# Attention scores with queries on partitions in place of keys, in a kernel of cluster attention and token mixing

## The chip, the cores and the metric

The kernel runs on one core of a Trainium2 chip. Its engines work side by side and each goes through its own queue of instructions in order: TensorE (PE; its weight loads are shown apart as PEld), VectorE (DVE), ScalarE (ACT), GpSimd (POOL), and SyncE (SP), which here only issues DMA transfers. The metric is the time of one execution on the device, in microseconds (us).

## The reference

Attention runs over 4 batches of 8 heads, 768 positions, 64 features. Queries and keys attend to one another only where both fall into the same one of 16 clusters of their head. The result, 4 x 768 x 512, goes through a mixer.

```python
q_assign = argmax(einsum('bhsd,hcd->bhsc', q_n, c_n))      # k_assign likewise
mask = q_assign[:, :, :, None] == k_assign[:, :, None, :]
scores = where(mask, scale * q @ k.T, -1e9)
scores = scores - max(scores, axis=-1)
attn = exp(scores)
attn = attn / (sum(attn, axis=-1) + 1e-09)
x = (attn @ v), heads side by side                          # (4, 768, 512)
theta = x @ w_theta
y = w_tok_r @ (x * cos(theta)) + w_tok_i @ (x * sin(theta))   # over positions
u = x + y
out = u + maximum(u @ w_ch, 0.0)
```

## The kernel before

**Two phases.** The attention fills the first 527 us, the mixer the rest. The attention goes over 16 pairs (a batch and two heads j = 0, 1), each in 12 units (`NU`), 192 in all.

**Scores.** A unit is one half `a` of the queries (384) by one key tile `i` (128 keys), for both heads. Scores stand transposed: keys on partitions, queries along the free axis (`scores`, L358). The products keep close to full float32 precision from parts: q and k are cut into a rounded part `hi` and a remainder `lo` (L297, L302), and SP spreads rows of these over the tiles `t1q`, `t2q`, `t1k`, `t2k` (`spread`, L308, 16 transfers a pair). Two matmuls then make one score tile `sc`: t1 over 112 rows, t2 over 128. Of the 112, 16 are the one-hot rows of the clusters, with a large constant, so that scores between different clusters are far below the others.

**The row of maxima.** With queries along the free axis the maximum over keys isn't at hand on any one engine. So the scores of queries by keys are also computed the other way round, from t1 alone, 11 units ahead (`LEAD`; `row_max`, matmul to `m` L329), and DVE takes the maximum of 768 (L333). These columns are transposed (`shift_row`, tile `mt`, L341), copied to `mr` and sent by SP into row 64 of `t2q` (L345, "t2q<-mr"), where a row of ones in `t2k` subtracts them from the scores by the matmul itself.

**After the scores.** ACT takes the exponential of 128x384 twice a unit into `at` (L362). POOL adds the `at` of the key tiles up in `acc` (L368). Three units later, every second unit, PE does the weighted sums of two units, `av` (L408), straight from `at`, since keys are on partitions as the product needs it. After the pair's last unit PE sums `acc` over partitions by a column of ones (`sums`, L377), and the sums go to DRAM (sd), back as 128 x 12 (sq), through DVE's reciprocal, to DRAM again and back as rows broadcast over partitions (rb): L388, L391, L395, L398, all on SP. POOL multiplies (`normalise`, L420), and the result goes to DRAM for the mixer.

**Preparation.** `assign` loads raw q and k of a pair (L224), makes the clusters' logits `lg` (L230), transposes them (`lt`, L239), takes maxima and one-hot rows on DVE, transposes them back (`ot`, L260), and SP puts the rows of `oht` into t1q and t1k (L268). Three sets of t tiles allow this two pairs ahead. Four weight matrices arrive as 64-bit floats; `to_f32` and `split_w` (L110 to L148) turn a chunk into float32 by four operations on ACT and DVE (L127 to L135) and into hi and lo on ACT and POOL. w_theta, a third of the token weights and w_ch are converted during the attention (`early_weights`), the others at the start of the mixer (`late`).

**The order.** The program is written unit by unit. Helpers that belong to a later unit wait in `todo` until it comes (`at_unit`, `stages` with one unit for each stage of a generator). `in_order` then chains all instructions of a unit to those of the unit before, engine by engine, so that each engine works in this order; SP is so chained only up to unit 5 (`SPU`), and after it in the order that the scheduler gives.

**Mixer.** `theta` (xp, tp, kk, r, ab, zh, zl) for each of 6 position tiles of 4 batches, `mix` (y, L672), `channel` (cp and cy, L695). The first channel matmul of the first batch comes 82 us after the last av; until then the late weights are converted.

Of the kernel before, what the change touches and what calls it, by code (L numbers as in the profile page):

```python
# [21 lines left out]
LEAD = 11  # L22
SPU = 6
A2 = (-4, 1, 3, 6, 8)
PRE = 4
PW = 256
TAIL = 2
WARM = 2
SUMS = (2, 2, 5, 8)
EARLY = 2  # L30
LAG = 3
NAT = 5
# [10 lines left out]
def kernel(  # L43
# [21 lines left out]
    P = 128  # L65
# [36 lines left out]
    ecol = cpool.tile([P, 32], F32, name="ecol")  # L102
    nc.vector.memset(ecol, 0.0)
    nc.vector.memset(ecol[:, 0:1], 1.0)


# [3 lines left out]
    def to_f32(src, cols, new):  # L110
# [17 lines left out]
        nc.vector.tensor_scalar(  # L128
# [30 lines left out]
    w_c = [hi_lo(wpool, f"wch{c}", DM) for c in range(NCT)]  # L159
# [14 lines left out]
    p3 = actx.enter_context(tc.tile_pool(name="p3", bufs=3))  # L174
    pw = actx.enter_context(tc.tile_pool(name="pw", bufs=2))
    p2 = actx.enter_context(tc.tile_pool(name="p2", bufs=2))
    p1 = actx.enter_context(tc.tile_pool(name="p1", bufs=1))
# [36 lines left out]
    def assign(pi):  # L214
# [5 lines left out]
        for n, src, eng in (("q", qT, nc.sync), ("k", kT, nc.scalar if pi == 0 else nc.sync)):  # L220

            raw = pw.tile([P, S], F32, tag="w64" if pi == 1 else "raw", name=f"raw{n}{pi}")
            st.setdefault(pi, dict(tsets[pi % 3]))["raw" + n] = raw
# [34 lines left out]
        for t in range(NT):  # L258
# [4 lines left out]
            out=oht, in_=ot, func=AF.Identity, scale=msc[0:4 * C], bias=mbi[0:4 * C])  # L263
        s = st[pi]
        for j in range(2):
            for n, x in enumerate(("t1q", "t1k")):
                g = 2 * C * n + C * j
                nc.sync.dma_start(out=f(s[x][96:96 + C, j]), in_=f(oht[g:g + C]))  # L268
# [3 lines left out]
    last_exp, last_acc, last_sum, last_load = ([None] for _ in range(4))  # L272
    KM = 96 + C

    def load_v(pi):
# [9 lines left out]
        q=(("t1q", 0, "hi", 0, 64), ("t1q", 64, "hi", 0, 32), ("t2q", 0, "lo", 0, 64), ("t2q", 96, "hi", 32, 32)),  # L285
        k=(("t1k", 0, "hi", 0, 64), ("t1k", 64, "lo", 0, 32), ("t2k", 0, "hi", 0, 64), ("t2k", 96, "lo", 32, 32)))


    for x in range(3):
        nc.gpsimd.memset(f(tsets[x]["t2q"][64:96]), 0.0)  # L290
        nc.gpsimd.memset(f(tsets[x]["t2k"][64:96]), 0.0)
        nc.gpsimd.memset(f(tsets[x]["t2k"][64:65]), 1.0)

    def part_hi(pi, n):
        s = st[pi]
        s["hi" + n] = pe.tile([P, S], F32R, tag="hi" + n, name=f"hi{n}{pi}")
        nc.scalar.copy(out=s["hi" + n], in_=s["raw" + n])  # L297

    def part_lo(pi, n, eng):
        s = st[pi]  # L300
        s["lo" + n] = s["raw" + n].bitcast(F32R)
        eng.tensor_tensor(out=s["lo" + n], in0=s["raw" + n], in1=f(s["hi" + n]), op=ALU.subtract)  # L302

    def spread(pi, n):
        s = st[pi]
        for to, row, part, first, rows in ROWS[n]:
            for j in range(2):
                nc.sync.dma_start(  # L308
                    out=f(s[to][row:row + rows, j]), in_=f(s[part + n][64 * j + first:64 * j + first + rows]))

    NU = 2 * NT

    def split_u(u):
        pi, x = divmod(u, NU)
        return (pi,) + divmod(x, NT)

    def row_max(u, c):


        pi, a, i = split_u(u)  # L320
        s = st[pi]
        t, j = divmod(i, 2)
        t += a * NT // 2
        if i == 0 and c == 0:
            s["nm", a] = p2.tile([P, 2, NT // 2], F32, tag="nm", name=f"nm{u}")
        if c == 0:
            s["m"] = ps0.tile([P, 2, 512], F32, tag="m", name=f"m{u}")
        m = s["m"]
        nc.tensor.matmul(  # L329
            m[:, c, 0:HS], lhsT=s["t1q"][0:KM, j, t * P:(t + 1) * P],  # L330
            rhs=s["t1k"][0:KM, j, c * HS:(c + 1) * HS], start=True, stop=True)
        if c == 1:
            nc.vector.tensor_reduce(  # L333
                out=s["nm", a][:, j, i // 2:i // 2 + 1], in_=m[:, :, 0:HS], op=ALU.max, axis=AX.XY,
                negate=True)

    def shift_row(pi, a):

        s = st[pi]
        mt = bank(f"mt{pi}{a}")[0:NT, 0:P]  # L340
        nc.tensor.transpose(out=mt, in_=s["nm", a].rearrange("p j t -> p (j t)"), identity=identf)  # L341
        mr = p2.tile([NT, P], F32R, tag="mr", name=f"mr{pi}{a}")
        nc.scalar.copy(out=mr, in_=mt)
        for j in range(2):
            (nc.scalar if pi == a == 0 else nc.sync).dma_start(  # L345
                out=f(s["t2q"][64:65, j, a * HS:(a + 1) * HS]).rearrange("o (t n) -> o t n", n=P),
                in_=f(mr[j * NT // 2:(j + 1) * NT // 2]))

    def scores(u, j):

        pi, a, i = split_u(u)
        s = st[pi]
        if j == 0:
            s["at", a, i] = p3.tile([P, 2, HS], F32, tag="at", name=f"at{u}", bufs=NAT)
        at = s["at", a, i]
        sc = bank(f"sc{u}_{j}")[:, 0:HS]
        for x, z, kk in (("t1k", "t1q", KM), ("t2k", "t2q", P)):
            nc.tensor.matmul(  # L358
                sc, lhsT=s[x][0:kk, j, i * P:(i + 1) * P],
                rhs=s[z][0:kk, j, a * HS:(a + 1) * HS],  # L360
                start=(x == "t1k"), stop=(x == "t2k"))
        last_exp[0] = nc.scalar.activation(out=at[:, j], in_=sc, func=AF.Exp, scale=SCALE)  # L362
        if j == 1:
            if i == 1:
                s["acc", a] = p2.tile([P, 2, HS], F32, tag="acc", name=f"acc{u}", bufs=3)
            if i > 0:
# [435 lines left out]
```

## Time and profile before

| | us |
|---|---|
| median of 3 runs | 879.95 (874.2 to 884.32) |
| the profiled execution | 885.43 |
| its span, first to last instruction | 883.6 |
| first matmul for maxima | 27.5 |
| first exp | 49.6 |
| last av of the attention begins | 524.1 (sixteen matmuls, 2.8) |
| first channel matmul of the first batch | 609.1 |

The profile is that of one execution. Its page lists for each group of instructions the busy time, the mean of one, and the idle time of the engine just before them with what ended most of it. Matmuls overlap, so the distance between their starts tells what one costs, more than its own duration. PEclk is the share of TensorE's clock that was granted; its mean over the execution was 0.959. The chain of waits is followed back from the last instruction of a window, at each step to what released it.

### The profile page before, as it was taken

The page shows a single profiled execution, that of the slowest core. Times are in us where ns is not written, and L with a number is a line of the kernel's source. Part 1 is how long each engine was busy: PE and PEld are TensorE (multiplying, and loading weights), DVE is VectorE, ACT ScalarE, POOL GpSimd, SP SyncE. Part 2 cuts the span into 40 slices and gives each one's busy share as a digit, 9 for nine tenths or more (in the row PEclk, how much of TensorE's full clock was granted, in tenths as well). Part 3 has the DMA queues.
Part 4 walks back from the last instruction along what each step waited for, and adds up shares of the span by engine and source line. Part 5 has one row for each costly group of instructions (what it writes and reads, how often), then busy time and mean ns, then how long its engine had stood idle before and what let it go on. Part 6 is the DMA issues. An engine that isn't in the chain of part 4 may idle for free.

```text
span 883.6 us, 12635 instructions
## 1 busy us (share of the span) xinstructions
PE 807.2 (91%) x4509; PEld 599.7 (68%) x4509; DVE 511.6 (58%) x664; ACT 400.6 (45%) x790; POOL 545.8 (62%) x337
## 2 busy tenths in 40 slices
PE   2699998998798898899899999889999999999998
PEld 0366555555565564565556658679988988899998
DVE  4486776766766776678465439995333432344222
ACT  2156653654555564466545565544233323332220
POOL 7177887988978987899788777466122412241231
PEclk9999998998988998999899999999999999999999
DMA  5875768655845754755563113520400040001002
GB/s 143 217 203 148 186 144 203 172 172 154 189 141 146 209 154 108 201 149 165 127 159 124 37 52 121 172 87 1 143 1 1 1 143 1 1 26 47 1 7 67
DMA packets 45903, 99.87 MB, mean 113 GB/s; under 512 B 12944, under 2 KB 17808, under 8 KB 45456
## 3 DMA queue, kind: packets, MB, share of 16 engines
q1 hardware_dynamic: 45684, 98.66, 40.4%
q8 instruction: 36, 0.59, 0.3%
q10 hardware_dynamic: 156, 0.40, 0.1%
q14 instruction: 27, 0.22, 0.1%
HBM read 45.25 MB, written 12.78 MB: 66 GB/s over the span
## 4 chain that ended last, share of the span: by engine, by line
PE 66%; DMA 9%; DVE 8%; POOL 6%; issue 5%; SPq 3%; ACT 2%; ACTq 0%; POOLq 0%; DVEq 0%
PE y L672 18%; PE sc L358 13%; PE av L408 11%; PE tp L605 6%; PE m L329 5%; PE cy L695 4%; POOL acc L368 3%; SPq L308 3%; DMA t2q<-mr 2%; PE cp L695 2%; DMA sd<-se 2%; DMA t1q<-hiq 1%; DMA rawk<-in_kT_dram 1%; DVE wtmp L135 1%; PE lg L230 1%
## 5 line engine op out<-in xcount | busy, mean ns | idle before, releaser
L362 ACT ACTIVATE at<-sc 128x384 f32<-128x384 f32 x384 | 182.0, 491 | 164.3 <-PE sc L358 152.7
L333 DVE TENSOR_REDUCE nm<-m 128x1 f32<-128x768 f32 x192 | 182.4, 953 | 125.8 <-PE m L329 121.3
L368 POOL TENSOR_TENSOR acc<-acc,at 128x768 f32<-128x768 f32 x128 | 242.3, 1893 | 20.0 <-ACT at L362 12.7
L358 PE MATMUL sc<-t2q,t2k 128*128 128x384 f32 x384 | 138.9, 362 | 36.6 <-DMA t2q<-mr 36.6
L408 PE MATMUL av<-at,vt 128*64 128x384 f32 x768 | 155.7, 530 | 0.0
L358 PE MATMUL sc<-t1q,t1k 112*128 112x384 f32 x384 | 147.6, 384 | 0.0
L329 PE MATMUL m<-t1k,t1q 112*128 112x384 f32 x384 | 141.8, 370 | 5.8 <-DMA t1k<-oht 4.8
L626 POOL TENSOR_TENSOR zlc<-ab,zhc 128x512 fp32r<-128x512 f32 x24 | 32.6, 1359 | 158.4 <-ACT zhc L624 158.2
L358 PEld LDWEIGHTS sc<-t1q,t1k 112*128 112x128 f32 x384 | 76.1, 198 | 54.0 <-issue 32.3
L358 PEld LDWEIGHTS sc<-t2q,t2k 128*128 128x128 f32 x384 | 76.6, 200 | 43.7 <-DMA t2q<-mr 43.6
L408 PEld LDWEIGHTS av<-at,vt 128*64 128x64 f32 x768 | 48.9, 142 | 63.6 <-issue 63.3
L368 POOL TENSOR_TENSOR acc<-at,at 128x768 f32<-128x768 f32 x32 | 59.1, 1848 | 51.4 <-ACT at L362 51.4
L329 PEld LDWEIGHTS m<-t1k,t1q 112*128 112x128 f32 x384 | 80.3, 209 | 9.1 <-issue 6.6
L609 DVE TENSOR_SCALAR kk<-tp 128x512 int32<-128x512 f32 x24 | 16.6, 690 | 99.1 <-PE tp L605 99.1
L686 POOL TENSOR_TENSOR ul<-xT,uh 128x384 fp32r<-128x384 f32 (+1 forms) x36 | 33.5, 956 | 38.1 <-ACT uh L685 35.8
L672 PE MATMUL y<-wi_lo,zhs 128*128 128x512 f32 (+1 forms) x216 | 52.3, 320 | 2.6 <-POOL wi_lo L145 2.6
L672 PE MATMUL y<-wi_hi,zhs 128*128 128x512 f32 (+1 forms) x216 | 52.4, 321 | 1.2 <-ACT wi_hi L144 1.2
L672 PE MATMUL y<-wr_hi,zhc 128*128 128x512 f32 (+1 forms) x216 | 53.0, 323 | 0.0
L672 PE MATMUL y<-wr_lo,zhc 128*128 128x512 f32 (+1 forms) x216 | 52.7, 322 | 0.0
L672 PE MATMUL y<-wr_hi,zlc 128*128 128x512 f32 (+1 forms) x216 | 52.6, 322 | 0.0
L672 PE MATMUL y<-wi_hi,zls 128*128 128x512 f32 (+1 forms) x216 | 52.5, 322 | 0.0
L600 ACT COPY xn<-xp 128x512 f32<-128x512 f32 x24 | 14.0, 585 | 83.5 <-PE xp L598 83.5
(140 smaller groups left out, 1398.6 us busy)
## 6 DMA issues: line engine op xcount, KB each, us to landing
rawq<-in_qT_dram SPq DMA_DIRECT2D x16, 384.0 KB
t1k<-hik SPq DMA_DIRECT2D x32, 192.0 KB
t2k<-hik SPq DMA_DIRECT2D x32, 192.0 KB
t1q<-hiq SPq DMA_DIRECT2D x32, 192.0 KB
t2q<-rawq SPq DMA_DIRECT2D x32, 192.0 KB
vt<-in_v_dram SPq DMA_DIRECT2D x16, 384.0 KB
rb<-sd SPq DMA_DIRECT2D x32, 192.0 KB
xT_d<-xt SPq DMA_DIRECT2D x16, 384.0 KB
```

The costliest lines, as they stand in the source:

```text
L308: nc.sync.dma_start(out=f(s[to][row:row + rows, j]), in_=f(s[part + n][64 * j + first:64 * j + first + rows]))
L329: nc.tensor.matmul(m[:, c, 0:HS], lhsT=s["t1q"][0:KM, j, t * P:(t + 1) * P], rhs=s["t1k"][0:KM, j, c * HS:(c + 1) * HS], start=True, stop= ...
L333: nc.vector.tensor_reduce(out=s["nm", a][:, j, i // 2:i // 2 + 1], in_=m[:, :, 0:HS], op=ALU.max, axis=AX.XY, negate=True)
L358: nc.tensor.matmul(sc, lhsT=s[x][0:kk, j, i * P:(i + 1) * P], rhs=s[z][0:kk, j, a * HS:(a + 1) * HS], start=(x == "t1k"), stop=(x == "t2k"))
L362: last_exp[0] = nc.scalar.activation(out=at[:, j], in_=sc, func=AF.Exp, scale=SCALE)
L368: last_acc[0] = nc.gpsimd.tensor_tensor(out=s["acc", a], in0=prev, in1=at, op=ALU.add)
L408: nc.tensor.matmul(s["av"][64 * j:64 * j + 64], lhsT=s["vt"][:, i, j, :], rhs=s["at", a, i][:, j], start=(i == 0), stop=(i == NT - 1))
L605: nc.tensor.matmul(tp, lhsT=xx[:, c, :], rhs=w_th[c][k], start=(n == 0), stop=(n == 3 * NCT - 1))
L626: nc.gpsimd.tensor_tensor(out=zl, in0=tr, in1=zh.bitcast(F32), op=ALU.subtract)
L672: nc.tensor.matmul(y_at(b, d, c0, c1), lhsT=zz[:, d * P:(d + 1) * P], rhs=ww[:, c0:c1], start=first and lead, stop=last, skip_group_check= ...
L686: nc.gpsimd.tensor_tensor(out=ul[:, d, :], in0=x, in1=uh[:, d, :].bitcast(F32), op=ALU.subtract)
L695: nc.tensor.matmul(cp, lhsT=w_c[d][k][:, e * P:(e + 1) * P], rhs=uu[:, d, :], start=(n == 0), stop=(n == 3 * NCT - 1), skip_group_check=True)
```

## The change

Scores stand with queries on partitions. A unit is a query tile `t` of a half `a` and one head `j`: four matmuls make 128 queries by 768 keys in a tile `m` of two banks (L344). DVE takes its maximum into a column (L353), ACT takes one exponential over 128x768 with this column as its bias and writes the sums of its rows beside it (L362). The separate matmuls for maxima, the shift row with its transfers, the additions on POOL and the sums on PE are gone. t2 has 96 rows in place of 128. Since the bias comes after the scale, POOL multiplies raw q by the scale beforehand (`scale_q`).

For the weighted sums keys have to be on partitions, so PE transposes the exponentials (`turn`, L375): twelve blocks of 128x128 for two units, into three banks (tr), which ACT (two) and DVE (one) copy to `aT`. The weighted sums (L388) follow a half later, one key tile of both heads per unit. The row sums of a half get a reciprocal on DVE, are transposed on PE (`rt`, L410), copied (rrow), written to DRAM (L415) and broadcast back (L419): one round trip in place of two, but for every half. DVE normalises while it reads av (L394).

Around this, other things move: two sets of t tiles in place of three, with the preparation of a pair 18 to 8 units ahead of it; SP is chained to the order of units throughout; the first pair's start is written in another order, with more idle matmuls; the first operation of the weight conversion (maximum and minimum) goes from DVE to POOL; and w_ch is converted in `late` rather than during the attention.

```diff
+TR = 3
+AV = 9
+RS = (7, 8, 9, 10)
+NAT = 6
+A_UNITS = (-18, -14, -13, -12, -11, -10, -8)
+SQ_UNIT = -16
+HI_UNITS = dict(q=-13, k=-12)
+LO_UNITS = dict(q=-12, k=-11)
+SP_UNITS = dict(q=-10, k=-8)
+V_UNIT = -2
+W_STEP = 22
+W_UNITS = (8, 14, 17, 20)
-WARM = 2
+WARM = 24
...
         nc.scalar.activation(out=w, in_=high.bitcast(F32), func=AF.Abs)
-        nc.vector.tensor_scalar(
+        nc.gpsimd.tensor_scalar(
             out=w, in0=w, scalar1=F64_LEAST, scalar2=F64_MOST, op0=ALU.max, op1=ALU.min)
...
-    for x in range(3):
-        x = (NPAIR + x) % 3
+    for x in range(2):
+        x = (NPAIR + x) % 2
...
+    def scale_q(pi):
+        nc.gpsimd.tensor_scalar_mul(st[pi]["rawq"], st[pi]["rawq"], SCALE)
...
+        m = s["m", a, t, j] = ps0.tile([P, 2, 512], F32, tag="m", name=f"m{u}")
+        for c in range(2):
+            for x, z, kk in (("t1k", "t1q", KM), ("t2k", "t2q", 96)):
                 nc.tensor.matmul(
-                    sm[32 * g:32 * g + 32], lhsT=ecol, rhs=s["acc", a][:, j], start=True, stop=True)
...
+                    m[:, c, 0:HS], lhsT=s[z][0:kk, j, q0:q0 + P],
+                    rhs=s[x][0:kk, j, c * HS:(c + 1) * HS],
+                    start=(x == "t1k"), stop=(x == "t2k"))
...
+        last_exp[0] = nc.scalar.activation(
+            out=at.rearrange("p (c n) -> p c n", c=2), in_=s.pop(("m", a, t, j))[:, :, 0:HS],
+            func=AF.Exp, bias=s["nm"][:, c:c + 1], scale=1.0, accum_out=s["ss"][:, c:c + 1])
+
+    def turn(g, bank_no):
...
+        for k in range(4):
+            j, i = divmod(4 * bank_no + k, NT)
+            nc.tensor.transpose(
+                out=bk[:, k * P:(k + 1) * P], in_=s["at", a, t, j][:, i * P:(i + 1) * P], identity=identf)
+        return (nc.vector.tensor_copy if bank_no == 2 else nc.scalar.copy), dict(
+            out=s["aT", a][:, 4 * bank_no:4 * bank_no + 4, t * P:(t + 1) * P],
+            in_=bk.rearrange("p (k n) -> p k n", k=4))
...
-        for c in range(NCT):
-            yield from split_w(*w_c[c], w_ch[c * P:(c + 1) * P], DM, raw_pair, nc.gpsimd, CKE)
...
+    while u < NUT + AV + HU or todo:
         start = len(nc.cur_bb.bb.instructions)
+        if u < NUT:
+            scores(u)
+            row_max(u)
+        copies = []
+        g, odd = divmod(u - TR, 2)
+        if 0 <= g < NUT // 2:
+            copies += [turn(g, x) for x in ((1, 2) if odd else (0,))]
+        h, i = divmod(u - AV, HU)
+        if 0 <= h < NUT // HU:
+            weighted(h, i)
+        for op, args in copies:
+            op(**args)
+        if u < NUT:
+            exps(u)
...
+        for c in range(NCT):
+            for gen in split_w(*w_c[c], w_ch[c * P:(c + 1) * P], DM, wt_pair, nc.gpsimd, CK):
+                run(gen)
+            if c % 2:
+                yield
```

On PE, near the end of the attention, two units read so before (sc is a score tile, m a tile for maxima of a later pair, av the weighted sums; the numbers behind a name tell buffers apart):

```order
L358 MATMUL sc_0_4818<-t1q_143,t1k_145 128x384
L358 MATMUL sc_0_4818<-t2q_144,t2k_146 128x384
L329 MATMUL m_4822<-t1k_145,t1q_143 128x384
L358 MATMUL sc_1_4824<-t1q_143,t1k_145 128x384
L358 MATMUL sc_1_4824<-t2q_144,t2k_146 128x384
L329 MATMUL m_4822<-t1k_145,t1q_143 128x384
L408 MATMUL av_4798<-at_4742,vt_4441 64x384 x2
L408 MATMUL av_4798<-at_4770,vt_4441 64x384 x2
```

This is one unit's scores for both heads, and av (four shown as two rows) for two units. After the change two units in a row read so (m now holds the scores, tr the transposed exponentials in banks 0 to 2):

```order
L344 MATMUL m_5309<-t1k_127,t1q_125 128x384
L344 MATMUL m_5309<-t2k_128,t2q_126 128x384
L344 MATMUL m_5309<-t1k_127,t1q_125 128x384
L344 MATMUL m_5309<-t2k_128,t2q_126 128x384
L375 MATMUL tr_1_5315<-identf,at_5241 128x128 x2
L375 MATMUL tr_1_5315<-identf,at_5257 128x128 x2
L375 MATMUL tr_2_5320<-identf,at_5257 128x128 x4
L388 MATMUL av_5300<-aT_5166,vt_5072 64x384 x2
L344 MATMUL m_5334<-t1k_127,t1q_125 128x384
L375 MATMUL tr_0_5340<-identf,at_5282 128x128 x4
L388 MATMUL av_5300<-aT_5166,vt_5072 64x384 x2
```

Two of a unit's six score-sized matmuls are gone, and twelve transposes have come in over two units; av goes with every unit. (Of the second unit's four score matmuls the first is shown.)

On SP, in the first fifth of its queue after the change, one pair's spreads (hiq, rawq, hik and rawk are the parts of q and k; the raw tiles hold lo by then), with the round trip of a half's sums (sd, rb) and the one-hot rows (oht) between those of q and those of k:

```order
L316 DMA t2q_126<-rawq_723 64x768 x2
L415 DMA sd_970<-rrow_933 6x128
L419 DMA rb_994<-sd_970 64x384 x2
L268 DMA t1q_125<-oht_942 16x768
L268 DMA t1k_127<-oht_942 16x768
L316 DMA t1k_127<-hik_884 64x768 x2
L316 DMA t2k_128<-hik_884 64x768 x2
L316 DMA t1k_127<-rawk_725 32x768 x2
L316 DMA t2k_128<-rawk_725 32x768 x2
L223 DMA rawq_1047<-in_qT_dram 128x768
L223 DMA rawk_1049<-in_kT_dram 128x768
```

The broadcast (rb) reads what the row ahead of it writes, so SP holds there until the write has landed; one-hot rows, k's spreads and the next pair's raw tiles stand behind it. (The rows of oht come twice, for both heads.) Before, the scheduler's order had t2q<-mr in this place, between the sums' transfers:

```order
L308 DMA t2k_132<-hik_1892 64x768 x2
L388 DMA sd_1992<-se_1990 4x384
L345 DMA t2q_137<-mr_1999 1x3x128
L308 DMA t1k_131<-rawk_1780 32x768 x2
L308 DMA t2k_132<-rawk_1780 32x768 x2
L391 DMA sq_1995<-sd_1992 128x12
L345 DMA t2q_137<-mr_1999 1x3x128
```

There the read of the sums (sq) holds SP until their write has landed, and the second transfer of maxima (mr) stands behind it.

More of the change, by code (lines that the diff above doesn't have):

```diff
@@ L499 @@
+    for _ in range(WARM):
+        nc.tensor.matmul(idle[:, 0:P], lhsT=identb, rhs=identb, start=True, stop=True)
     run(g0)
[L500 to L501 removed]
     load_v(0)
[L503 to L514 removed]
```

279 lines of the change are left out of this document (115 added, 164 removed).

## The prediction

> **What bounds the kernel now.** I read the page's engine totals and costliest groups first, then a table of windows, then the chain of waits over one border between pairs. Totals and four groups (line, engine, operation, tiles, shapes, count, busy us and mean ns, idle time before them and its releaser):
>
> ```profile
> PE 807.2 (91%) x4509; PEld 599.7 (68%) x4509; DVE 511.6 (58%) x664; ACT 400.6 (45%) x790; POOL 545.8 (62%) x337
> L362 ACT ACTIVATE at<-sc 128x384 f32<-128x384 f32 x384 | 182.0, 491 | 164.3 <-PE sc L358 152.7
> L333 DVE TENSOR_REDUCE nm<-m 128x1 f32<-128x768 f32 x192 | 182.4, 953 | 125.8 <-PE m L329 121.3
> L368 POOL TENSOR_TENSOR acc<-acc,at 128x768 f32<-128x768 f32 x128 | 242.3, 1893 | 20.0 <-ACT at L362 12.7
> L600 ACT COPY xn<-xp 128x512 f32<-128x512 f32 x24 | 14.0, 585 | 83.5 <-PE xp L598 83.5
> ```
>
> PE is busy 91% of the span; ACT and DVE mostly wait for it. POOL alone is a second candidate, with 1.9 us of additions in most units. The windows (window, length, busy us of PE, PEld, DVE, ACT, POOL, then the granted clock, the DMA share and GB/s) say where that matters:
>
> ```profile
> 200.00:300.00 100.00, 88.89 (x464) 55.02 (x465) 70.03 (x72) 54.53 (x112) 85.50 (x45) 0.88 0.63 166
> 400.00:525.00 125.00, 120.55 (x652) 76.91 (x652) 66.48 (x77) 69.87 (x149) 102.92 (x57) 0.97 0.41 113
> 525.00:612.00 87.00, 78.13 (x401) 64.38 (x398) 76.35 (x117) 48.13 (x90) 52.23 (x38) 0.94 0.32 101
> 612.00:884.00 272.00, 268.48 (x1681) 246.84 (x1679) 92.90 (x166) 78.97 (x138) 71.69 (x66) 1.00 0.10 36
> ```
>
> From 612 on PE is full at full clock, and the change leaves that stage's PE work alone. In 200 to 300 PE idles 11% and runs the rest at 0.88 of its clock. The chain there (start, us, what) shows why:
>
> ```profile
> 234.62 6.85 DMA sd<-se
> 241.49 0.33 SPq L391
> 241.87 1.71 DMA t2q<-mr
> 243.62 0.69 PE sc L358
> ...
> 244.63 2.76 PE av L408 x8
> ...
> 250.62 1.44 PE av L408 x8
> ...
> 252.26 0.45 PE ot L260 x6
> 252.71 0.78 PE lg L230 x8
> ...
> 254.76 0.33 PE lt L239 x3
> ...
> 268.39 5.10 DMA sd<-se
> ```
>
> Scores stand still until the row of maxima (t2q<-mr) is in place, and that small transfer stands on SP behind a read that waits for the sums' first write (sd<-se). It comes back in the next pair. After the wait the eight av matmuls take 2.76 us, six us later 1.44: a stretch at half clock follows the stall, as 0.88 in the window says. So a border is paid for twice: the window's 11 us idle and 0.12 of its clock, over some 3.3 pairs, are up to 7 us a pair.
>
> **What the change does to PE.** First its cadence (start, duration, engine, line; durations overlap, so starts count), in the clean stretch before the last pairs and in the mixer:
>
> ```profile
> 485.72 0.34 PE L358 MATMUL sc<-t1q,t1k 112*128 112x384 f32 x1
> 485.89 0.34 PE L358 MATMUL sc<-t2q,t2k 128*128 128x384 f32 x1
> 486.07 0.34 PE L329 MATMUL m<-t1k,t1q 112*128 112x384 f32 x1
> 486.34 1.51 PE L408 MATMUL av<-at,vt 128*64 128x384 f32 x8
> 487.79 0.27 PE L341 MATMUL mt<-identf,nm 128*6 128x128 f32 x1
> ...
> 649.01 0.60 PE L598 MATMUL xp<-identf,xT 128*128 128x128 f32 x4
> 649.36 1.17 PE L605 MATMUL tp<-wth_hi,xh 128*128 128x512 f32 x4
> ```
>
> A 384-column matmul starts 0.18 us after the one before (485.72 to 486.07), 0.27 where the shape changes (486.07 to 486.34). The removed part is one m pass per unit, 2 x 0.18. What stays is four score matmuls (0.72, or 0.81 with one change of shape) and av: 1.44 per two units, 0.72, which I take as 0.78 since it now comes unit by unit. New are twelve transposes of 128x128 per two units. Their nearest row is xp: four from 649.01 to 649.36, and with three the lt piece of 0.33, so 0.09 to 0.11 each; I take 0.108, the dearer, as their input is fresh too: 0.65 per unit. A unit becomes 0.81 + 0.65 + 0.78 = 2.24 us (before: six matmuls of 0.18 and av, 1.88). 192 units: 431. To it 15 assignments of 0.78 + 0.33 + 0.45 = 1.6 each, 24, and 32 small transposes of reciprocals at 0.11, 4. PE work of the attention: 459, where before a clean pair needs 12 x 1.88 + 1.6 and the sums' matmuls, about 25, and 16 of them 400. So PE is charged some 60 us more, and the stalls above are what this can be paid from.
>
> The Trainium skill ("TensorE: Matmul & The Clock Gate", Part 4) gives about 275 ns for such a transpose in a kernel; that is the single transpose (mt 0.27 above), not the pitch of a row of them, and by it the term would be 1.65 us per unit and the kernel some 190 us longer. The xp row has four in 0.35, so the row decides.
>
> **What it does to the other engines.** A unit of 2.24 us gets on DVE one maximum (0.95), half a copy of 128x512 from PSUM (L600 on ACT 0.585; a DVE read of that size is between the same 0.585 and 0.95 for 768) and a share of the assignment, about 1.6; on ACT one exp of 128x768 (two halves now take 0.98; one instruction saves a start, so 0.80 to 0.98), one copy (0.585), a share of casts, about 1.7. Both are under 2.24, and each exp is wanted only three units later. The loop that closes soonest is that of the two maxima buffers: maximum and exp (0.95 + 0.98) have to end within the 3.7 us in which PE does the rest of this unit and the next; 1.7 us to spare, so no cost until something holds DVE or ACT for longer (the conversions, below). POOL loses its additions (242 us in L368's row, and its second form) and stops being near the bound; scaling q there adds one pass over 128x768 per pair, 1 to 1.9 us by the additions' row. Bias and accumulated sums inside exp are in no row; I take nothing, at most the 0.18 that separates 0.98 from 0.80, which ACT hides.
>
> **Start.** Scores of the first unit and first exp before:
>
> ```profile
> 27.53 0.66 PE L329 MATMUL m<-t1k,t1q 112*128 112x384 f32 x1 [4.82 <-DMA t1k<-oht]
> ...
> 49.55 2.15 ACT L362 ACTIVATE at<-sc 128x384 f32<-128x384 f32 x4 [1.76 <-PE sc L358]
> ...
> 524.09 2.80 PE L408 MATMUL av<-at,vt 128*64 128x384 f32 x16
> ...
> 609.13 0.51 PE L695 MATMUL cp<-uh,wch_hi 128*128 128x384 f32 x2
> ```
>
> The 22 us from 27.5 to 49.6, in which only the eleven units of maxima ran ahead while SP issued two more pairs' transfers, go. The first scores wait for the same one-hot rows as m did; two of the four transfers move to ACT's queue and save their issue (0.59 each): about 25.5 (24 to 28). The first transposes need exps three units late: 3 us. After the last scores copies and av of the last half trail by about 5. The last av ends without stalls at 25.5 + 459 + 3 + 5 = 492, against 526.9 now.
>
> **Stalls that remain.** SP is now in the order of the units always, so its waits hold all that stands behind. An issue of SP from the timeline, one of its waits (sum, times, longest) and two landings from the chain, all of before:
>
> ```profile
> 254.30 0.59 SPq L268 DMA_DIRECT2D t1q<-oht  x1
> ...
> SPq L398 <- DMA sd<-sq: 32.7, 16, 3.7
> ...
> 38.61 5.61 DMA rawk<-in_kT_dram
> ...
> 290.08 3.76 DMA t1q<-hiq
> ```
>
> Between the reciprocals of a half (unit -10 of a pair) and the next pair's logits (lg, unit -2 on the same count) SP must issue the write of the sums (0.6), wait for it (2.0 on the mean of the L398 row, at most 3.7), issue two broadcasts (1.2), four one-hot rows (2.4) and eight spreads of k (8 x 0.6 = 4.9), and then the raw tiles, whose buffer the k spreads must have read (2 to 3.8, the t1q landing), and which take 3.5 to 5.6 to land (the rawk piece is the one of a full queue). Sum 16.6 to 20.6; PE's eight units are 18.0 to 19. The logits are late by nothing to 3 us a pair; with 0.8 in the mean, 15 x 0.8 = 12. Behind them on PE stand the next scores, so it is a stall of all. Before, pairs were prepared two ahead and so this was covered; with two tile sets in place of three nothing else covers it.
>
> Of the weight conversion the first operation moves from DVE to POOL, and DVE's shift right behind it now waits for POOL, with the next maxima queued behind it. On POOL it may stand behind the new scaling of q, which waits for the raw tile, and behind the subtraction of q or k, 1.9 us each:
>
> ```profile
> L302 POOL TENSOR_TENSOR rawq<-rawq,hiq x16: 1812/1936/2521, 14.8 to 443.7; 128x768 fp32r<-128x768 f32 x16
> ...
> L128 DVE TENSOR_SCALAR wtmp<-wtmp x16: 345/361/1473, 533.7 to 591.2; 128x384 f32<-128x384 f32 x16
> ```
>
> Two maxima buffers give PE under 3 us of cover. One or two of eight conversions meet the wait for q (4 us), the others one subtraction at most: 10 us in all (0 to 20). Four us for the rest of the queues. The last av then ends at 492 + 12 + 10 + 4 = 518.
>
> **Transition.** From 526.9 to the first channel matmul (609.1) is 82.2, in which DVE is the busiest (76.35 of 87 above), with the late weights' four operations per chunk. One of them leaves DVE (16 chunks x 0.36 to 1.47, by the L128 row), but eight w_ch chunks come in: 8 x 3 operations of 0.3 to 0.5 at two thirds of the length, about +8 on DVE; on POOL 24 first operations and eight subtractions, +25 to +35, where it was busy 52 of 87. In DVE's order the last w_ch operations stand ahead of the first channel output, and the channel needs w_ch itself. The thetas of the first batch start earlier against the last av. I take +5 (-5 to +20): 87. The L128 row spreads from 345 to 1473 ns for one shape. The Trainium skill ("SBUF — State Buffer", the shared port pair) has the later of a DVE and a POOL instruction fully blocked for the whole of the other, and the row's spread agrees; by it the move would only swap who holds the port, and the 6 us that 16 x 0.36 takes off DVE would come back as waits.
>
> **Sum.** 518 + 87 + 274.5 (609.1 to 883.6, unchanged) = 879.5; the profiled execution lasted 885.43 with a span of 883.6, so 881.3 of its own time, 4.1 less. It stood 0.6% above the median (879.95), so 875.9 against that: **876**. The unknowns (logits 0 to 30, conversion 0 to 20, transition -5 to +20, start -1.5 to +2.5) make 862 to 892 for this case.
>
> **Rivals.**
> - All stalls covered: raw tiles land in 3.5 us and the sums' write in 2, so logits are in time; POOL, freed of additions, takes the first operation at once. No 12, no 10: 876 - 22 = 854, and with the transition at its better end 844. For it: the 6.85 and 5.10 us of the chain came from SP behind two DRAM round trips of the sums, of which one stays, and POOL is freed; against it: the logits' slack by the sum above is about nothing. Chance 0.27.
> - The other side: the raw tiles land in 5.6 and the logits are 3 to 4 us late each pair, and as after the 6.85 us wait above, PE then runs the next two units at half clock (2.76 against 1.44 for av: about 1.7 lost per stall). 15 x (3.3 + 1.7) = 75 in place of 12: about 938; with half of the pairs hit, 907. It decides from the point where the SP sum passes nine units, 20.2 us. Chance 0.18.
> - The transition: POOL's extra 30 us and w_ch at the end of DVE's queue hold the channel, +20 instead of +5: 891. Chance 0.11.
> - Transposes do not keep the clock up. 29% of a unit would be transposes; if the clock stayed at 0.5 throughout, 459 more of PE time, about 1300. The xp rows in the mixer run at full clock, but among many matmuls. The Trainium skill (same page, Part 4) says that transposes don't count as busy for the clock in the same way; no stage before has this share of them. Chance 0.03.
> - That it does not do what it says: none of the removed work can stay, as its rows are gone from the program. No chance given.
>
> **The numbers.** Forecast 0.41. The range takes the first rival from 845 on and the second up to 912: outside lie about 0.05 below, and 0.08 + 0.03 + 0.02 above. What a measurement here can tell from no change is about 1%: 871 to 889. Of the forecast case 0.15 lies below 871 and 0.05 above 889, of the transition rival 0.07. Faster 0.27 + 0.15 = 0.42, same 0.21 + 0.04 = 0.25, slower 0.05 + 0.07 + 0.18 + 0.03 = 0.33.
>
> **What would show it.** Right: pairs of about 30 us with PE over 92% busy and m four times per unit at 0.18; waits "PE lg <- DMA rawq or rawk" of about 12 us, no wait for a maxima row; last av near 518; DVE waits for POOL's wtmp near 10 us; first channel matmul near 605. Transposes at 0.108. Wrong: lg waits over 40 us with a clock below 0.9 (the second rival); none at all (the first); PE waiting for aT or for a free bank, which I priced at nothing; a channel that waits for wch_lo by more than 15 us; transposes at 0.27 each.

## The result: slower by 5.5%

The changed kernel takes 928.3 us (927.7 to 929.4, 4 runs) against 880.6 for the kernel before: 1.055 of its time, 95% interval 1.049 to 1.061. The forecast was 876, range 845 to 912, so the time lies above the range. The profiled execution took 927.7 us with a span of 925.9.

| us from the start of the span | before | forecast | after |
|---|---|---|---|
| first matmul for maxima or scores | 27.5 | 25.5 | 21.1 |
| last av ends | 526.9 | 518 | 552.6 |
| first channel matmul of the first batch | 609.1 | 605 | 648.5 |
| end | 883.6 | 879.5 | 925.9 |

The start came earlier than forecast, and every stage after it took longer: against the forecast the last av ends 35 us late, the transition takes 9 us more, and the stage behind it, which I had called unchanged, 3 more. From the page after the change, the totals and the groups that answer to those shown of before:

```profile
PE 855.8 (92%) x5129; PEld 644.7 (70%) x5129; DVE 534.2 (58%) x835; ACT 492.1 (53%) x911; POOL 285.6 (31%) x205
L353 DVE TENSOR_REDUCE nm<-m 128x1 f32<-128x768 f32 x192 | 182.5, 952 | 130.8 <-PE m L344 129.9
L362 ACT ACTIVATE at<-m,nm 128x768 f32<-128x768 f32 x192 | 173.3, 903 | 80.9 <-DVE nm L353 63.9
L375 PE MATMUL tr<-identf,at 128*128 128x128 f32 x1152 | 161.9, 277 | 2.4 <-DVE aT L522 2.4
L291 POOL TENSOR_SCALAR rawq<-rawq 128x768 f32<-128x768 f32 x15 | 32.2, 2146 | 163.3 <-DMA rawq<-in_qT_dram 157.6
```

PE is as full as before with more work in it. POOL's busy time has fallen from 545.8 to 285.6 us, and the time did not fall with it. The windows of the changed kernel (columns as before):

```profile
25.00:50.00 25.00, 20.18 (x115) 16.45 (x116) 15.71 (x22) 16.62 (x33) 5.74 (x3) 0.80 0.57 156
...
200.00:300.00 100.00, 96.09 (x587) 61.92 (x586) 65.90 (x99) 67.48 (x127) 21.44 (x12) 0.98 0.55 151
...
400.00:500.00 100.00, 92.27 (x545) 59.63 (x544) 64.92 (x96) 64.69 (x120) 24.67 (x12) 0.93 0.56 153
500.00:560.00 60.00, 60.00 (x354) 39.74 (x353) 35.20 (x54) 38.01 (x72) 7.18 (x5) 1.00 0.29 99
560.00:655.00 95.00, 72.60 (x381) 61.38 (x379) 84.66 (x119) 48.80 (x98) 87.37 (x66) 0.93 0.28 86
```

In 200 to 300 PE was busy 88.9% at 0.88 of its clock before and is busy 96.1% at 0.98 now: the stalls at the borders are paid back there. That window is one of the better ones. Over most of the attention (first row before, second after) the gain is smaller, since new stalls came, as in 400 to 500:

```profile
50.00:500.00 450.00, 410.31 (x2188) 259.31 (x2187) 311.81 (x329) 249.64 (x519) 382.81 (x205) 0.93 0.60 160
50.00:500.00 450.00, 426.21 (x2555) 275.68 (x2556) 297.85 (x448) 301.96 (x563) 108.42 (x56) 0.96 0.55 150
```

PE goes from 91% at 0.93 to 95% at 0.96. A pair still takes longer, since the work itself grew: from 500 to 560 PE is full at full clock, and three tenths of a unit's time are transposes (next).

**The pitch of a unit.** PE's timeline in a clean stretch:

```profile
329.65 0.44 PE L344 MATMUL m<-t1k,t1q 112*128 112x384 f32 x1
...
330.47 0.60 PE L375 MATMUL tr<-identf,at 128*128 128x128 f32 x4
331.00 0.87 PE L388 MATMUL av<-aT,vt 128*64 128x384 f32 x4
331.80 0.44 PE L344 MATMUL m<-t1k,t1q 112*128 112x384 f32 x1
...
332.61 1.04 PE L375 MATMUL tr<-identf,at 128*128 128x128 f32 x8
333.58 0.87 PE L388 MATMUL av<-aT,vt 128*64 128x384 f32 x4
334.38 0.44 PE L344 MATMUL m<-t1k,t1q 112*128 112x384 f32 x1
```

Two units take 334.38 - 329.65 = 4.73 us, 2.37 each. Scores are 0.82, close to the forecast (0.81). Four transposes take 0.53 and eight 0.97: 0.11 apiece plus 0.1 for the change to av behind them. av takes 0.80.

**A stall.** One of the places where PE stands still, in the chain of waits:

```profile
418.84 0.80 ACT w L128
...
419.72 2.79 POOL w L129
...
422.54 0.56 DVE w L131
423.10 0.88 DVE nm L353
...
424.06 1.00 ACT at L362 x2
...
425.10 1.65 PE m L344 x4
```

This is a weight conversion. POOL needs 2.79 us for its new operation, DVE's shift waits for it, the next maximum stands behind the shift on DVE, the exp waits for the maximum, and PE has no free m tile until 425.10. PE's timeline there:

```profile
425.10 0.69 PE L344 MATMUL m<-t1k,t1q 112*128 112x384 f32 x1 [3.01 <-ACT at L362]
...
426.54 1.05 PE L375 MATMUL tr<-identf,at 128*128 128x128 f32 x4
```

PE stood still for 3.0 us, and the four scores then take 1.44 us (425.10 to 426.54) in place of 0.82: half clock, granted from 424.2 to 431.0. The waits of the whole execution say how often, and that another wait of the forecast isn't there (sum, times, longest):

```profile
DVE w L131 <- POOL w L129: 30.2, 8, 4.4
...
PE cp L697 <- ACT uh L687: 11.5, 1, 11.5
...
PE m L344 <- ACT at L362: 10.7, 7, 3.0
...
PEld lg L229 <- POOL rawq L291: 3.1, 2, 2.5
```

All eight conversions of the attention make DVE wait, and PE has a gap behind each of them (0.6 to 3.9 us, 17 in sum); behind five of these gaps it runs at half clock for 3.4 or 6.8 us, 27 in sum. The logits (lg) wait for raw tiles twice in all. And there is one wait of 11.5 us at the first channel matmul. DVE and PE around it:

```profile
642.23 1.40 DVE L685 TENSOR_TENSOR xT<-y,xT 128x256 f32<-128x256 f32 x4
643.56 0.41 DVE L134 SCALAR_TENSOR_TENSOR wtmp<-wtmp 128x256 int32<-128x256 int32 x1
...
648.06 0.29 DVE L131 TENSOR_SCALAR wtmp<-wtmp 128x256 int32<-128x256 int32 x1 [0.42 <-POOL wtmp L129]
...
648.54 1.01 PE L697 MATMUL cp<-uh,wch_hi 128*128 128x384 f32 x2 [11.54 <-ACT uh L687]
```

PE has done the last y at 637 and waits for u = x + y. DVE's additions (L685) stand between w_ch conversions (wtmp) until 643.6. Even then the cast of u (uh, L687) doesn't begin before 647.98: ahead of it in ACT's queue stands a cast of w_ch (wch_hi, 647.67), which waits for DVE's conversion in turn. So w_ch holds the channel on two queues, DVE's and ACT's.

### The profile page after: what moved, and what is told of

Same layout as the page of the kernel before. It is cut to its first block, busy times and chain, and to the rows that moved or that the text cites. A ratio compares the mean times of both kernels' runs of the same rounds, so it can differ in the third digit from the quotient of the medians.

```text
span 925.9 us, 14005 instructions
## 1 busy us (share of the span) xinstructions
PE 855.8 (92%) x5129; PEld 644.7 (70%) x5129; DVE 534.2 (58%) x835; ACT 492.1 (53%) x911; POOL 285.6 (31%) x205
## 4 chain that ended last, share of the span: by engine, by line
PE 46%; DVE 9%; POOL 2%; issue 2%; ACT 1%; DMA 1%; DVEq 0%; ACTq 0%; POOLq 0%; SPq 0%
PE y L674 16%; PE av L388 6%; PE m L344 6%; PE tp L608 5%; PE tr L375 4%; PE cy L697 4%; PE cp L697 2%; DVE wtmp L134 2%; DVE wtmp L131 2%; DVE wtmp L136 1%; PE y L697 1%; PE xp L601 1%; DMA wtmp<-in_wrT_dram 1%; DVE nm L353 1%; POOL w L129 1%
## 5 line engine op out<-in xcount | busy, mean ns | idle before, releaser
L353 DVE TENSOR_REDUCE nm<-m 128x1 f32<-128x768 f32 x192 | 182.5, 952 | 130.8 <-PE m L344 129.9
L362 ACT ACTIVATE at<-m,nm 128x768 f32<-128x768 f32 x192 | 173.3, 903 | 80.9 <-DVE nm L353 63.9
L344 PE MATMUL m<-t1k,t1q 112*128 112x384 f32 x384 | 154.4, 402 | 16.9 <-ACT at L362 10.7
L388 PE MATMUL av<-aT,vt 128*64 128x384 f32 x768 | 169.5, 523 | 0.0
L375 PE MATMUL tr<-identf,at 128*128 128x128 f32 x1152 | 161.9, 277 | 2.4 <-DVE aT L522 2.4
L522 ACT COPY aT<-tr 128x512 f32<-128x512 f32 x192 | 112.5, 586 | 90.6 <-PE tr L375 88.9
L375 PEld LDWEIGHTS tr<-identf,at 128*128 128x128 f32 x1152 | 140.7, 144 | 12.5 <-issue 1.8
L344 PEld LDWEIGHTS m<-t1k,t1q 112*128 112x128 f32 x384 | 75.5, 197 | 105.9 <-ACT aT L522 68.7
L344 PE MATMUL m<-t2k,t2q 96*128 96x384 f32 x384 | 134.9, 351 | 0.0
L291 POOL TENSOR_SCALAR rawq<-rawq 128x768 f32<-128x768 f32 x15 | 32.2, 2146 | 163.3 <-DMA rawq<-in_qT_dram 157.6
L344 PEld LDWEIGHTS m<-t2k,t2q 96*128 96x128 f32 x384 | 76.4, 199 | 0.0
L522 DVE COPY aT<-tr 128x512 f32<-128x512 f32 x96 | 65.8, 685 | 1.6 <-PE tr L375 1.5
L388 PEld LDWEIGHTS av<-aT,vt 128*64 128x64 f32 x768 | 39.1, 137 | 34.2 <-issue 31.4
L309 POOL TENSOR_TENSOR rawq<-rawq,hiq 128x768 fp32r<-128x768 f32 x15 | 27.4, 1826 | 102.8 <-PE tr L375 72.7
```

The source lines that it names most:

```text
L291: nc.gpsimd.tensor_scalar_mul(st[pi]["rawq"], st[pi]["rawq"], SCALE)
L344: nc.tensor.matmul(m[:, c, 0:HS], lhsT=s[z][0:kk, j, q0:q0 + P], rhs=s[x][0:kk, j, c * HS:(c + 1) * HS], start=(x == "t1k"), stop=(x == "t ...
L353: nc.vector.tensor_reduce(out=s["nm"][:, c:c + 1], in_=s["m", a, t, j][:, :, 0:HS], op=ALU.max, axis=AX.XY, negate=True)
L362: last_exp[0] = nc.scalar.activation(out=at.rearrange("p (c n) -> p c n", c=2), in_=s.pop(("m", a, t, j))[:, :, 0:HS], func=AF.Exp, bias=s ...
L375: nc.tensor.transpose(out=bk[:, k * P:(k + 1) * P], in_=s["at", a, t, j][:, i * P:(i + 1) * P], identity=identf)
L388: nc.tensor.matmul(s["av"][64 * j:64 * j + 64], lhsT=s["vt"][:, i, j, :], rhs=s["aT", a][:, j * NT + i], start=(i == 0), stop=(i == NT - 1))
```

## The experiments

Each theory had one of the three losses: A, the conversion's first operation on POOL; C, the place of w_ch; E, the changes between kinds of matmul on PE. Rivals stand in the expectations.

**The first operation back on DVE.**

```diff
-        nc.gpsimd.tensor_scalar(
+        nc.vector.tensor_scalar(
             out=w, in0=w, scalar1=F64_LEAST, scalar2=F64_MOST, op0=ALU.max, op1=ALU.min)
```

> The changed kernel, with the first operation of the weight conversion (maximum and minimum) back on DVE everywhere, so that no DVE instruction waits for POOL in the middle of a conversion. Theory A (eight conversions in the attention each stop DVE behind POOL's 1.9 to 2.8 us operation, PE waits 1 to 4 us and then runs 3.4 to 6.8 us at half clock): the PE gaps at conversions go, 20 us of gaps and some 13 us of clock, less 8 x 0.5 us of DVE work that comes back; last av near 523 in place of 552.6, total 890 to 905. Rival B (DVE is short of time in a conversion whoever does the first operation, as it has three more operations in any case): the gaps stay, total 920 to 930. In the transition the move takes 16 + 8 operations off POOL and puts them on DVE: up to 10 us longer if DVE bounds it, the same or shorter if POOL and DVE hold each other up.

898.1 us (1.022 of the kernel before, 1.017 to 1.027), 30 less than the changed kernel. The last av ends at 528.4 in place of 552.6, the first channel matmul comes at 620.3 in place of 648.5, so the transition is 91.9 in place of 95.9. From 50 to 500 the clock is 0.99 in place of 0.96. (The means over the whole executions, 0.989 and 0.965, don't compare: in this run the clock's records begin only at 35 us, and the 384-column matmuls ahead of them start 0.32 us apart in place of 0.18, so the half clock of the start isn't counted.) Of DVE's 30 us of waits in the attention this is left:

```profile
DVE w L129 <- ACT w L128: 9.8, 7, 2.4
```

Theory A holds, a little below its size (24 us at the last av, 30 expected); rival B falls. The longest gaps of PE left at conversions are 1.6 us near 121 and 1.9 near 463. There DVE's own first operation took 1.52 and 1.42 us, against 0.43 and 0.56 where it met nothing: POOL's subtraction for k (L309) was under way as it began, and it ended 0.3 and 0.4 us after that subtraction.

**The same in the attention alone.** Late conversions keep POOL for it (a test on the caller chooses `nc.vector` or `nc.gpsimd`).

> As the run before, but only for the conversions in the attention; the late ones in the mixer keep their first operation on POOL. Theory A: last av as in the run before, near 523, total 890 to 905. The difference of the two runs is the transition alone: if the late conversions gain from POOL's help, this one is 5 to 10 us faster than the run before; if the two engines hold each other up, it is the same or slower.

900.6 us (1.026, 1.022 to 1.030), 2.5 more than the run before. The programs of the two are the same up to the last av, which came at 523.9 here and 528.4 there: a pair of such runs differs by this much in the attention. The first channel matmul came at 620.5 and 620.3, so in the transition POOL's help gave nothing back; a gain of 5 us is excluded, whether it costs 0 or 5 isn't settled.

**w_ch in the attention again**, together with the first operation on DVE.

```diff
+    w_c = [hi_lo(wpool, f"wch{c}", DM) for c in range(NCT)]
...
+        for c in range(NCT):
+            yield from split_w(*w_c[c], w_ch[c * P:(c + 1) * P], DM, raw_pair, nc.gpsimd, CKE)
...
-W_STEP = 22
+W_STEP = 15
-NAT = 6
+NAT = 5
```

(and the loop over w_ch taken out of `late`.)

> First operation on DVE everywhere and, beside that, w_ch converted during the attention again (twelve conversions, one every 15 units; five buffers for the exponentials in place of six, for room). Theory C (the w_ch conversions stand ahead of the first channel in DVE's queue and hold it, PE waits 11.5 us for uh): transition from last av to first channel matmul 10 to 14 us shorter than in the first run, attention longer by 4 conversions x 1 us; total 880 to 897, 8 us below the first run. Rival D (the transition is bound by the token weights on DVE and POOL, w_ch only fills gaps): 0 to 4 us below the first run or above it.

893.2 us (1.018, 1.014 to 1.021), 4.9 below the first run. Last av 533.8 (5.4 later, four conversions), first channel matmul 617.3: the transition is 83.5 against 91.9. And from there to the end 274.1 us are left against 277.5, as before the change (274.5): with w_ch late, the channel itself was held up too. The mechanism of theory C is there, 8.4 + 3.4 us, but 5.4 of it come back in the attention (about as much as the 4.5 by which the two runs before this one differ there). The transition is also no shorter than before the change (82.2), so what is over is w_ch's and not the token weights'. Rival D falls by this, not by the total, whose 4.9 lies between what the two had expected.

**Weighted sums in twos.**

```diff
-            weighted(h, i)
+            if i % 2:
+                weighted(h, i - 1)
+                weighted(h, i)
```

> The changed kernel with the weighted sums of two units in a row every second unit, as the kernel before had them, and the rest as it is. Theory E (a unit on PE costs 2.37 us rather than the forecast 2.24 because each change between scores, transposes and weighted sums costs 0.1 us): two changes fewer in two units, 96 x 0.2 = 19 us less, total about 909. Rival F (the changes hide beside something else, or the later sums make stalls elsewhere): 925 to 930.

905.7 us (1.032, 1.028 to 1.036), 22.6 below the changed kernel. PE's timeline:

```profile
325.23 0.42 PE L344 MATMUL m<-t1k,t1q 112*128 112x384 f32 x1
...
326.03 0.60 PE L375 MATMUL tr<-identf,at 128*128 128x128 f32 x4
326.38 0.42 PE L344 MATMUL m<-t1k,t1q 112*128 112x384 f32 x1
...
327.18 1.04 PE L375 MATMUL tr<-identf,at 128*128 128x128 f32 x8
328.15 1.51 PE L388 MATMUL av<-aT,vt 128*64 128x384 f32 x8
329.59 0.83 PE L229 MATMUL lg<-rawq,cb 128*32 128x384 f32 x2
```

Four transposes ahead of scores take 0.35, not 0.53, and eight av 1.44, not twice 0.80: two units take 4.36 us instead of 4.73. 96 x 0.37 would be 36; 27 arrive at the last av. PE's gaps up to there (those over 0.3 us, summed from the trace) are 38 us against 35, and half-clock stretches cost 20 us against 26; so some 10 of the 36 are missing, and where they went stays open. Theory E holds.

**All three.**

> The changed kernel with all three edits at once: first operation of the conversion on DVE, w_ch converted in the attention, weighted sums of two units in a row. If the three causes are separate, their gains add: 928 - 30 (first operation) - 5 (w_ch) - 22 (changes of shape) = 871, between 865 and 880, that is level with the kernel before or just below. If they share a cover (the longer units hid DVE's conversions), the sum is smaller: 880 to 893.

878.6 us, ratio 0.9997 (0.997 to 1.002): level with the kernel before. One by one they gave 30.2, 4.9 (on top of the first) and 22.6, in sum 57.7; together 49.7, within the first band expected. So these three are what made the change slower, and without them it is neither faster nor slower.

**The price of the transposes, from both sides.** First without them and without their copies; av reads a tile of constants, so the attention's result is left out and only its time is of use.

```diff
-            s["aT", a] = p3.tile([P, 2 * NT, HS], F32, tag="aT", name=f"aT{g}")
+            s["aT", a] = fixed
+        return None
```

> The changed kernel without the transposes of the exponentials and without their copies to SBUF: the weighted sums read a constant tile instead, so the attention's result is not the attention's. PE's unit falls from 2.37 to about 1.62 us. Theory E (PE's pitch sets the attention, the copies are hidden): last av 192 x 0.75 = 144 us earlier at the most, and what DVE and ACT then allow (maximum 0.95, exp 0.9 and its read-out 0.2 a unit, under 1.62 together with the rest) leaves 100 to 144 of it: total 785 to 830. Rival I (the copies on ACT and DVE and the loop of two maxima buffers set the pitch): less than 100 gained, with waits of PE for exps in place of the transposes, 830 to 870.

885.8 us in the profiled execution (a second one took 1360.2; it has no trace, and what happened there stays open). The last av ends at 507.9, only 44.7 earlier, though the pitch holds 192 x 0.75 = 144 us of transposes. Both expectations were too low in time. In kind it is rival I: less than 100 us gained, and waits for exps in place of the transposes. The waits:

```profile
ACT at L362 <- DVE nm L353: 190.4, 155, 8.9
...
PEld m L344 <- ACT at L362: 84.7, 106, 5.8
...
PE lg L229 <- POOL rawq L291: 26.1, 9, 4.4
```

PE now waits for the m tiles (scores, maximum, exp) and, at nine borders, up to 4.4 us for the scaled q of the next pair; from 50 to 500 the granted clock falls from 0.96 to 0.88. Then each transpose twice:

```diff
-            nc.tensor.transpose(
-                out=bk[:, k * P:(k + 1) * P], ...
+            for _ in range(2):
+                nc.tensor.transpose(
+                    out=bk[:, k * P:(k + 1) * P], ...
```

> The changed kernel with each transpose of the exponentials made twice over, into the same place. The last run without them gained 45 us in the attention, not 144, because other waits came up (logits, sums). If PE alone sets the pitch from here upwards, 1152 more transposes of 0.108 us lengthen the attention by the whole 124 us, less what the present gaps take in (up to 20): 1025 to 1055. If the same waits still set part of it, 60 to 100: 990 to 1025.

1019.7 us, last av at 646.4: 93.8 later for 1152 transposes. The window's row shows PE full:

```profile
50.00:600.00 550.00, 543.59 (x3685) 392.60 (x3684) 307.89 (x463) 304.04 (x585) 110.54 (x57) 0.99 0.46 127
```

1152 x 0.108 = 124. PE's gaps over 0.3 us fall from 35 to 15 us, and what half-clock stretches cost falls from 26 to 10: the extra work filled about 35 us of waits. The time lies at the upper end of the second band expected. So more transposes cost three quarters of themselves (94 of 124 us), but the transposes as they are could give back only 45 us, because PE then waits for the maxima loop and for the scaled q at the end of SP's chain.

**The chain on SP, without transposes.** As the run before last, with k's spreads issued from ACT's queue.

```diff
-            at_unit(u + SP_UNITS[n], spread, pi, n)
+            at_unit(u + SP_UNITS[n], spread, pi, n, ("hi", "lo"), nc.scalar if n == "k" else None)
```

> The kernel without transposes and copies again (weighted sums of a constant tile, so not the attention's result), and the eight transfers that spread k issued from ACT's queue instead of SP's. Theory J (without transposes the chain on SP from a half's sums over one-hot rows and k's spreads to the next pair's raw tiles is the bound: logits late by 4 us a pair, each with 3 to 5 us at half clock behind it): 4.9 us leave the chain, the logits come in time, attention 50 to 80 us shorter than without transposes alone, total 805 to 840. Rival K (the conversions' first operation on POOL and the loop of maxima and exps hold it): within 20 us of the run without transposes, 865 to 890.

935.2 us, 49 more than the one execution without this edit. Waits of PE for q's logits are gone, as theory J said; but it did not see what eight issues do on ACT:

```profile
234.00 1.67 ACTq L316 DMA_DIRECT2D t1k<-rawk  x2
236.07 2.02 ACTq L316 DMA_DIRECT2D t2k<-rawk  x2
238.14 0.90 ACT L362 ACTIVATE at<-m,nm 128x768 f32<-128x768 f32 x1 [5.86 <-DMA t1k<-rawk]
```

The exps stand 5.9 us behind the issues and PE behind them, once in nearly every pair and with half clock after it. How much SP's chain alone costs the kernel without transposes is therefore not measured.

**The kernel before, without its queueing.** What the forecast said of the borders before is tested on the kernel before: the row of maxima goes out from ACT's queue.

```diff
-            (nc.scalar if pi == a == 0 else nc.sync).dma_start(
+            nc.scalar.dma_start(
                 out=f(s["t2q"][64:65, j, a * HS:(a + 1) * HS]).rearrange("o (t n) -> o t n", n=P),
```

> The kernel before, with the transfers of the row of maxima issued from ACT's queue for every pair, so that they no longer stand on SP behind the reads of the sums. Theory G (what the kernel before lost at the borders of pairs was this queueing, as the forecast said): the waits of the scores for the row of maxima (36.6 us) and most of the 31 us of clock lost behind them go, less 64 issues of 0.6 us on ACT, which has room: 825 to 855. Rival H (POOL's additions, 85% busy, or another transfer is late next): 865 to 880.

863.8 us, 0.983 of the kernel before (0.977 to 0.988). In 50 to 500 the clock is 1.00 where it was 0.93, and PE no longer waits for the row of maxima:

```profile
50.00:500.00 450.00, 412.41 (x2289) 257.90 (x2290) 324.94 (x340) 254.04 (x540) 385.02 (x211) 1.00 0.56 161
```

The time lies between the two bands expected, just below rival H's. Up to the last av, PE's gaps over 0.3 us sum to 40 us against 42 before, while what the recorded half clock costs there falls from 31 to 2: it is the clock that came back, and new gaps took the place of the old. What is late next is neither POOL nor another transfer but ACT, which issues:

```profile
198.41 1.43 ACTq L345 DMA_DIRECT2D t2q<-mr  x2
199.94 1.70 ACT L362 ACTIVATE at<-sc 128x384 f32<-128x384 f32 x4 [1.56 <-PE sc L358]
```

Each two issues hold ACT for 1.4 us, and the scores wait about 1 us for a free bank, twice a pair. So only the half that had stood behind the read of the sums:

```diff
-            (nc.scalar if pi == a == 0 else nc.sync).dma_start(
+            (nc.scalar if a == 1 or pi == 0 else nc.sync).dma_start(
```

> The kernel before, with the row of maxima issued from ACT's queue for the second half of each pair only, whose transfers are the ones that stood behind the read of the sums; the first half stays on SP. With both halves on ACT each pair of issues held ACT for 1.4 us, and the scores waited 0.9 to 1.1 us for a bank at each: of 32 such waits 16 go. Expected 863.8 - 16 = 848, between 842 and 858. If the first half is held up on SP too, 862 to 875.

859.5 us, 0.976 of the kernel before (0.972 to 0.980). It beats both kernels, by 21 and 69 us. Over the run before it gains 4 us and not the 16 expected, and the two intervals overlap: seven waits of PE of 1.7 to 3.5 us came up at other places of the attention.

## Why the prediction was wrong, step by step

- **What bounds the kernel before: right in kind.** At the borders stood the queue on SP and the half clock behind it. Up to the last av, PE's gaps and the half clock are 42 + 31 us, under 5 a pair where the forecast had up to 7 from one window. Not all of it can be had: moving two transfers of each pair gives 21 us, because other waits come up. POOL at 85% was no bound at 880, since the kernel got 21 us shorter with the same additions.
- **The stalls at the borders go: right.** PE is busy 96% at 0.98 in the window that had 89% at 0.88. Over 50 to 500 it is only 95% at 0.96; with the conversions' first operation back on DVE it is 98% at 0.99.
- **PE's pitch: the step that failed first.** Forecast 2.24, measured 2.37. The transposes cost 0.108 as taken from the row of the mixer. What was mis-sized is the change from one kind of matmul to the next: I counted one per unit (0.09) and 0.06 within av; the change from transposes to av, 0.1 to 0.18 each time, was not in the sum. 192 x 0.125 = 24 us. The row for it stood in the prediction (0.27 instead of 0.18 at 486.07).
- **Conversions: the second step that failed, 10 us forecast, 24 measured.** "10 us in all (0 to 20)", of which "one or two of eight meet the wait". All eight do: POOL's operation is 1.9 us for 512 columns and 2.8 for 768, I had priced the wait by what stands ahead of it on POOL and not by its own length, which is more than the 1.7 us that the maxima loop has to spare. And I added no half clock behind these waits, though I had shown one. Measured: 24 us at the last av in the first experiment, 28.7 in the second, whose attention is the same program.
- **SP's chain: 12 forecast, about 3 found.** (Its sum of 16.6 to 20.6 took the mean of 2.0 for the sums' write at both ends; with the longest, 3.7, the upper end is 22.2.) The longer pitch gave it room; in the kernel without transposes the same wait appears, 26 us of it. The mechanism is real, but it wasn't on the path here, and the rival built on it (logits late by 3 to 4 us) came true in its time by chance, 928 against 907 to 938, and not in its cause.
- **Start: 4.4 us better than forecast**, and lost again at once: PE runs at half clock up to 35 us (0.80 from 25 to 50), which costs at most 5. The forecast had added no half clock here; and the logits at 49 wait 1.8 us for the scaled q, so a faster start would not have kept all of it.
- **Transition: +5 forecast, +13.8 measured**, 95.9 against 82.2 from last av to first channel, and 3 more behind it, which I had held fixed. By the experiments 8.4 of the 13.8 went with w_ch; 4.0 went with the first operation on POOL in the first experiment, which the second leaves open (0 to 5). The place was named (w_ch ahead of the channel in DVE's order), and the rival of the transition, +20, was nearer than the forecast. That POOL's help would gain nothing on DVE agrees with the second experiment, in which POOL's share made no difference at the first channel matmul. The spread of the L128 row goes with POOL, as the prediction read it: in the trace of before, each of its six long operations in the transition (1.0 to 1.5 us) began under a POOL instruction and ended 0.2 us after one. It isn't every overlap, though: two operations of 0.35 us ran under a POOL instruction that went on for 1.5 us more.
- **A clock held down by transposes: refuted for this mix.** With three tenths of PE's time in transposes the clock is 1.00 from 500 to 560, and with twice as many 0.99 from 50 to 600. The Trainium skill ("TensorE: Matmul & The Clock Gate", Part 4) has it that transposes don't count as busy in the same way. No loss by this shows here, where a row of transposes lasts at most 1.84 us and stands between other matmuls; what transposes alone would do, no run shows.

In the forecast's sum: -4.4 at the start, +24 pitch, +14 conversions, -9 SP's chain, +9 transition, +3 behind it, together about 36.5 of the 46.5 us by which the span missed. The 10 left lie in the attention. The low clock at the start is up to 5 of them, and up to 5 more if the conversions are taken at 28.7; how much of either is real stays open.

## What to carry to other kernels

When a step moves to another engine, price the wait of the engine it leaves by the whole length of the moved step on its new engine, against the spare time of the tightest loop behind it, and add the half-clock stretch that follows a PE stall. Price a new kind of matmul by its changes of kind as well as by its count. And before a redesign that is paid from stalls, look for the one queue that makes them: here two transfers of each pair, moved to another queue, gained 21 us, where the redesign with its three losses taken out only broke even.

## What was not expected of the hardware

- POOL's maximum-and-minimum over 128x768 took 2.78 us, its multiplication by a constant over the same size 2.15, against 1.83 for its subtraction of two tensors of this size.
- The exp with sums is two instructions on ACT: 0.80 us to the start of the next and 0.19 for reading the sums out.
- Gaps of PE of 1.3 to 2 us were already followed by 3.4 or 6.8 us at half clock in some places of the changed kernel (1.5 us at 191.0, 2.0 at 244.5, 1.3 at 305.1), and not in others (2.0 at 364.6).
